# Block sums of a weight moved to the first wave, a seven-product step in one more wave, loads in one row and gated casts

## The chip, the cores and the metric

One core of one Trainium2 chip. The kernel is one launch; its time is device microseconds (us), from the runs of that one core. Three runs of the kernel before gave 197.93, 197.23 and 197.22 us, median 197.23. All other times come from one profiled execution. Its span, from the first instruction to the last, is 196.2 us, and that execution took 197.88 us as a whole.

Engines: PE (TensorE, matrix products), DVE (VectorE), ACT (ScalarE), POOL (GpSimd), SP (SyncE, which here only issues transfers). "SPq" in a row is SP's queue of transfer issues.

## The reference, cut to what matters

A decayed linear attention over 4 batches of 8 heads, 768 positions, head size 64, feeds a two-layer network of 3072 tokens, 512 to 2048 to 512:

```
for b in range(nb):                       # 64 positions at a time
    intra = (einsum(qb, kb) * Dmask) @ vb
    inter = (qb * lam_pow) @ kv_state
    out[:, :, sl] = intra + inter
    kv_state = lam_block * kv_state + einsum(kb * rev_pow, vb)
...
x = out.transpose(0, 2, 1, 3).reshape(B * S, H * D)
h = x @ w_in
g = h * sigmoid(1.702 * h)
return g @ w_out
```

## The kernel before

The work runs in six waves of 512 tokens, w = 0 to 5. Waves 0 and 1 hold two batches with 256 positions each; waves 2 to 5 hold all four batches with 128 positions each. Wave w does the network for its own tokens, and in between the attention of wave w+1, so that its input xT is there when the next wave begins.

**The first product** (x @ w_in, 16 blocks of 128 columns). A plain block, `mlp1`, is four matmuls of 512 columns. The other form works on a group of four blocks and half blocks of x (256 tokens): seven products (`in_product`, n = 1 to 7, two columns of blocks, two steps each, so four matmuls of 256 columns a product) in place of eight, in the manner of Strassen and Winograd. It needs two sorts of sums made by DVE: four sums of blocks of w_in for each group (`in_sums(g)`, lines 510 to 519, kept in the tiles `w_in_t`), and four sums of half blocks of x for each wave (`x_sums`, line 528, tiles `x_s`). After the products DVE or ACT copy three of the seven banks to `part`, DVE adds the others up (line 551, `h_sb`), and ACT takes the activation (line 562). `GR[w]` names the groups that wave w does in this form; before, wave 2 does groups 2 and 3 so and the other eight blocks plain, waves 3 to 5 do all four groups so. Which group holds which blocks is in `GROUPS`; w_in is loaded in five chunks (`IN_CH`), groups 1, 2 and 3 lie in chunks 0 to 3, group 0 in chunks 1 and 4.

**The second product** (g @ w_out) takes the seven-product form from wave 1 on (`product`, line 460; sums of g by DVE in `g_sums`, line 439; results added by DVE at line 484 or copied by ACT at 482, then stored by SP, lines 490 and 492). Wave 0's second product is plain (`mlp2`), its stores are issued late, in wave 1 (line 580).

**Attention of waves 2 to 5**: k and q are loaded (`load`, line 88), multiplied by powers (`do_cast`, line 209; on DVE for wave 2, on POOL for waves 3 to 5: the steps K0, K1, Q0, Q1), turned by a transposing DMA that SP issues (`turn_dma`, line 245: tk0, tk1, tq0, tq1), then come the scores (S0 to S3, line 335), masks (M or m), states and outputs (R), and the copy to xT. v is cast by ACT (v0, v1).

**What sets the order.** In waves 0 and 1 a list of main items (products) runs with a list of side items, each with the number of the main item ahead of which it is placed: `IN_SUMS_AT`, `X_AT`, `L_AT` are such places in wave 1. Main item 12 of wave 1 is a plain block, item 26 and 27 are the two halves of product 4, 28 and 29 of product 3. In waves 2 to 5 the order is written out by hand in `STEPS`: lower-case a to d with a number is a product of group 1 to 4 of that wave, capital A to D an activation, f a plain block, i the sums of w_in of one group, P a product of the second layer, g its sums, o the output of product 2, X the sums of x for the next wave, L the loads for the wave after the next (Lk: k and q, Lv: v). Each engine runs its instructions in this order and each waits only for what it needs; SP's loads, turns and stores share one queue in this order too.

Buffers that matter: k and q are loaded into one buffer each, v into two. `h_sb`, `o_sb` share a tag of six buffers; a buffer is free again when its add, activation or store has been done.

Of the kernel before, what the change touches and what calls it, by code (L numbers as in the profile page):

```python
# [25 lines left out]
def kernel(  # L26
# [21 lines left out]
    G = W // P  # L48
# [194 lines left out]
    def turn_dma(w, c, nm):  # L243
        y = work.tile([P, 2 * NP, P], bf16, tag=f"{nm}T{c}", bufs={"k": 1, "q": 2}[nm], name=f"{nm}T")
        nc.sync.dma_start_transpose(out=y, in_=cast[w, c, nm].rearrange("p b c -> p (b c)"))
        trans[w, c, nm] = y
# [149 lines left out]
    def mlp1(w, fc):  # L396
        if w not in g_of:
            g_of[w] = gp.tile([P, FFC, W], bf16, tag="g", name="g_sb")
        j, i = w_in_of[fc]
        h = acc("ps_h", shape=[P, W], tag="mm")  # L400
        for kc in range(KC):
            nc.tensor.matmul(h, w_in_sb[j][:, kc, i * P : (i + 1) * P], xT[w][:, kc, :],  # L402
                             start=(kc == 0), stop=(kc == KC - 1))
        nc.scalar.activation(g_of[w][:, fc, :], h, GELU)  # L404
# [88 lines left out]
                out=out.rearrange("(b s) d -> s b d", s=S)[w * P : (w + 1) * P, 2 * i + t.start : 2 * i + t.stop, cols],  # L493
                in_=o[:, t])

    GR = {w: (2, 3) if w == 2 else (1, 2, 0, 3) for w in range(2, 6)}
    TAGS = {w: ("aQXV", "aXVQ") if w == 2 else ("aQXV", "mXVQ", "aQXV", "aXVQ") for w in range(2, 6)}
    IN_SUMS_AT, X_AT, L_AT = ((13.5, 2), (26.5, 3)), 28.5, ((12, "v"), (24, "kq"))
    GROUPS = (((4, 13), (14, 15)), ((0, 2), (1, 3)), ((6, 5), (8, 7)), ((10, 9), (12, 11)))
    USED = sorted({g for w in range(NW) for g in GR.get(w, ())})  # L500
    TI = {g: [const.tile([P, KC // 2, 2, P], bf16, name=f"w_in_t{g}{n}") for n in range(1, 5)] for g in USED}
    x_sum, h_part, h_bank, h_out = {}, {}, {}, {}

    def in_half(g, kh, j, u):
        ch, i = w_in_of[GROUPS[g][u][j]]
        return w_in_sb[ch][:, 2 * kh : 2 * kh + 2, i * P : (i + 1) * P]

    def in_pair(g, kh, j):
        (ch, a), (_, b) = (w_in_of[GROUPS[g][u][j]] for u in range(2))
        return w_in_sb[ch].rearrange("p kc (i f) -> p kc i f", f=P)[:, 2 * kh : 2 * kh + 2, a : b + 1 : b - a]  # L510

    def in_sums(g):
        whole_pair = all(w_in_of[GROUPS[g][0][j]][0] == w_in_of[GROUPS[g][1][j]][0] for j in range(2))
        for u in (None,) if whole_pair else (0, 1):
            t1, t2, t3, t4 = (t if u is None else t[:, :, u] for t in TI[g])
            b11, b12, b21, b22 = (in_pair(g, kh, j) if u is None else in_half(g, kh, j, u)
                                  for kh in range(2) for j in range(2))
            for o, x, y in ((t1, b12, b11), (t2, b22, t1), (t3, b22, b12), (t4, b21, t2)):
                nc.vector.tensor_tensor(o, x, y, op=SUB)  # L519
# [38 lines left out]
    def in_gelu(w, g, n, bank=None):  # L558
        bank = bank or h_out.pop((w, g, n))
        i, j = {2: (0, 0), 3: (0, 1), 4: (1, 0), 5: (1, 1)}[n]  # L560
        a, b = (GROUPS[g][u][j] for u in range(2))
        nc.scalar.activation(g_of[w][:, a : b + 1 : b - a, 256 * i : 256 * i + 256], bank, GELU)  # L562
# [30 lines left out]
    def one_step(w, s):  # L593
        if s[0] == "+":
            w, s = w + 1, s[1:]
        x, a = w + 1, s[1:]
        if s[0] == "f":
            mlp1(w, int(a))
        elif s[0] in "abcd":
            k = "abcd".index(s[0])  # L600
            in_product(w, GR[w][k], int(s[1]), TAGS[w][k], dve_copy if s[2:] == "v" else act_copy)
        elif s[0] in "ABCD":
            in_gelu(w, GR[w]["ABCD".index(s[0])], int(a))
        elif s[0] == "P":
            product(w, int(s[1]), (int(s[2]),))
        elif s[0] in "kq":
            do_cast(x, int(a), s[0], nc.vector)
        elif s[0] in "KQ":
            do_cast(x, int(a), s[0].lower(), nc.gpsimd)
        elif s[0] == "t":  # L610
            turn_dma(x, int(s[2]), s[1])
        elif s[0] == "v":
            cast_v(x, int(s[1]), ((act_copy, dve_copy)[s[2:] == "v"],))
        elif s[0] == "S":
            n_scores(x, int(a))
        elif s[0] == "M":
            n_masks(x, int(a))
        elif s[0] == "m":
            n_masks(x, int(a), True)
        elif s[0] == "R":  # L620
            n_rest(x)
        elif s[0] == "o":
            c11.pop(w)()
        elif s[0] == "X":
            x_sums(x)
        elif s[0] == "i":
            in_sums(int(a))
        elif s[0] == "g":
            m0, m1 = {"l": (0, 4), "h": (4, 8)}[s[1]]
            g_sums(w, m0, m1, tuple(int(c) - 1 for c in s[2:]))  # L630
        elif s[0] == "L":
            load(w + 2, {"v": "v", "k": "kq"}[a])
        else:
            raise ValueError(s)

    STEPS = {
        2: ("f0 f1 a1 f2 a7 a2 i1 f3 K0 tk0 b1 a6 b7 i0 f4 A2 a5 b2 b6 K1 tk1 a4 A5 f13 a3 A4 B2 b5 gl12 Q0 "
            "tq0 b4 f14 B5 b3 B4 Q1 tq1 Lv f15 gl3 P10 P11 gh31 S0 S1 M0 P20 M1 gh2 P21 v0 P70 P71 S2 S3 M2 "
            "M3 v1 o P60 gl4 gh4 P61 Lk R P50 P51 P40 X P41 P30 P31 "),
        3: ("a1 a7v a2 a6 K0 tk0 b1 b7v A2 a5 b2 b6 a4 A5 a3 c1 A4 K1 tk1 B2 b5 c7v c2 c6 B5 b3 b4 d1v Q0 "  # L640
            "tq0 c5 B4 C2 d7v d2 d6 D2 c3 c4 Q1 tq1 Lv d5 d4 P10 C4 d3 C5 D4 P11 gl3 D5 gh3 S0 S1 M0 P20 m1 "
            "gl1 P70 P71 gl2 P21 v0 gh12 S2 S3 M2 m3 v1 o P40 P60 gl4 gh4 P61 Lk R P50 P51 X P41 P30 P31 "),
        4: ("a1 a7v a2 a6 K0 tk0 b1 b7v A2 a5 b2 b6 a4 A5 a3 c1 A4 K1 tk1 B2 b5 c7v c2 c6 B5 b3 b4 d1v Q0 "
            "tq0 c5 B4 C2 d7v d2 d6 D2 c3 c4 Q1 tq1 d5 d4 P10 C4 d3 C5 D4 P11 gl3 D5 gh3 S0 S1 M0 P20 m1 gl1 "
            "P70 P71 gl2 P21 v0 gh12 S2 S3 M2 m3 v1 o P40 P60 gl4 gh4 P61 R P50 P51 X P41 P30 P31 "),
        5: ("a1 a7v a2 a6 b1 b7v A2 a5 b2 b6 a4 A5 a3 c1 A4 B2 b5 c7v c2 c6 B5 b3 b4 d1v c5 B4 C2 d7v d2 d6 "
# [4 lines left out]
    def gate_pool(x):  # L651
        nc.gpsimd.tensor_copy(behind_q, x)
# [4 lines left out]
    with tc.manual_schedule():  # L657
# [87 lines left out]
        side, main = [(0, (end, 0, 1))], []  # L745
        for w in range(ND):
            n = len(main)
            main += mlp_items(w)
            e = len(main)
            x = w + 1  # L750
            if x < ND:
                for c, (k_at, q_at, v_at, k_turn, q_turn, s_at, e_at) in enumerate(
                        ((19, 20, 19, 24, 25.5, 27, 30), (26.5, 28, 28, 29, 30, 32, 34))):
                    side += [(n + k_at, (do_cast, x, c, "k", (nc.vector, nc.gpsimd)[c])),
                             (n + q_at, (do_cast, x, c, "q", nc.vector)),
                             (n + v_at, (cast_v, x, c, ((pool_copy, pool_copy), (act_copy, act_copy))[c])),
                             (n + k_turn, (turn_pe, x, c, "k", act_copy)),
                             (n + q_turn, (turn_pe, x, c, "q", act_copy)),
                             (n + s_at, (start, x, c)), (n + e_at, (end, x, c))]
            elif x == ND:  # L760
                for c in range(HF):
                    tk, tq = n + 2.1 + 2 * c, n + 4 + c
                    side += [(tk, (do_cast, x, c, "k", nc.vector)), (tk, (turn_dma, x, c, "k")),
                             (tq, (do_cast, x, c, "q", nc.vector)), (tq, (turn_dma, x, c, "q")),
                             (n + 17 + 2 * c, (cast_v, x, c, (act_copy,)))]
                side += [(n + 7, (stores,))]
                side += [(n + 16, (n_two, x, 0)), (n + 20, (n_two, x, 1)), (n + 24, (n_rest, x))]
                side += [(n + t, (in_sums, g)) for t, g in IN_SUMS_AT] + [(n + X_AT, (x_sums, x))]
            if w == 0:
                side += [(n + 14, (weight_sums, j)) for j in range(NCH - 1)]  # L770
            else:
                side += [(n + 7.5, (weight_sums, NCH - 1))]
                side += [(n + 8.9, (g_sums, w, 0, 4)), (n + 12.9, (g_sums, w, 4, 6)), (n + 15.9, (g_sums, w, 6, 8))]
            side += [(n + 12, (load, w + 2))] if w == 0 else [(n + t, (load, w + 2, nms)) for t, nms in L_AT]
# [8 lines left out]
        for w in range(ND, NW):  # L783
            for s in STEPS[w].split():
                one_step(w, s)
# [30 lines left out]
```

## Time and profile before

| what | value |
|---|---|
| median of three runs | 197.23 us |
| the profiled execution: whole, span | 197.88 us, 196.2 us |
| PE busy | 188.5 us (96%) |
| DVE busy | 147.3 us (75%) |
| ACT busy | 120.4 us (61%) |
| POOL busy | 42.7 us (22%) |
| granted TensorE clock | 1.00 throughout |
| a plain block of four 512-column matmuls, start to start | 0.86 us |
| a product of four 256-column matmuls, start to start | 0.44 us |
| starts of the first product of waves 2, 3, 4, 5 on PE | 80.97, 111.51, 139.93, 168.38 us |

A matmul is pipelined: its row shows a duration longer than the distance to the next one, so distances between starts are what counts on PE. Times in views are us from the span's start. In a row of the timeline of an engine, the first number is the start, the second the length of the row, "xN" the instructions merged in it, and the bracket the idle time before it with what ended it.

### The profile page before, as it was taken

What the parts mean: (1) busy time and instruction counts of PE and PEld (TensorE: products, weight loads), DVE (VectorE), ACT (ScalarE), POOL (GpSimd) and SP (SyncE); (2) the same over time, 40 slices, a digit from 0 to 9 for tenths busy, and PEclk for the clock granted to TensorE, in tenths of its full rate; (3) what the DMA queues carried; (4) which work ended last, traced back from release to release, by engine and by line L of the source; (5) the groups of instructions that cost most, each with busy time, mean ns of one, the idle gap of its engine ahead of it and who ended that gap; (6) DMA issues with size and microseconds to landing.
All of it is one profiled execution on the core that took longest, in us unless ns stands there. A gap on an engine that the chain in (4) does not pass through costs nothing.

```text
span 196.2 us, 5312 instructions
## 1 busy us (share of the span) xinstructions
PE 188.5 (96%) x2201; PEld 142.7 (73%) x2201; DVE 147.3 (75%) x277; ACT 120.4 (61%) x225; POOL 42.7 (22%) x62
## 2 busy tenths in 40 slices
PE   7999999999999999997999999999999899999993
PEld 2567544456784789764788888878888788888882
DVE  1795036288799894999899679799879796789850
ACT  4958663056676725374946278895288975487711
POOL 4579000051000000891000294000392000000000
PEclk9999999999999999999999999999999999999999
DMA  5999999999998699998902999953999101400113
GB/s 145 335 248 188 202 205 223 271 295 269 244 235 199 144 226 241 211 234 194 212 5 68 214 288 176 223 113 87 231 307 212 27 0 57 160 5 0 34 62 122
DMA packets 89086, 33.90 MB, mean 173 GB/s; under 512 B 67430, under 2 KB 88422, under 8 KB 89062
## 3 DMA queue, kind: packets, MB, share of 16 engines
q1 hardware_dynamic: 84164, 28.84, 62.5%
q0 software_dynamic: 4896, 4.72, 14.4%
q8 instruction: 17, 0.28, 0.6%
q14 instruction: 7, 0.06, 0.1%
q10 hardware_dynamic: 2, 0.00, 0.0%
HBM read 27.26 MB, written 6.29 MB: 171 GB/s over the span
## 4 chain that ended last, share of the span: by engine, by line
PE 67%; DMA 18%; DVE 7%; SPq 2%; POOL 2%; ACT 1%; issue 1%; DVEq 0%; ACTq 0%
PE ps_X L460 17%; PE ps_hX L543 10%; PE ps_V L460 8%; DMA w_out<-in_moe_w_out_dram 7%; PE ps_h L402 6%; PE ps_hV L543 5%; PE ps_Q L460 4%; PE ps_h L414 4%; DMA kf<-in_k_dram 4%; PE ps_out L571 3%; DMA vf<-in_v_dram 3%; PE ps_hQ L543 3%; DVE w_in_t L519 3%; DMA qT<-qs 3%; DMA qf<-in_q_dram 2%; PE ps_o L390 2%
## 5 line engine op out<-in xcount | busy, mean ns | idle before, releaser
L460 PEld LDWEIGHTS <-g_s 128*128 128x128 bf16 x320 | 30.6, 98 | 4.6 <-DVE g_s L439 0.4
L209 POOL TENSOR_TENSOR ks<-kf,k_pow 128x512 bf16<-128x512 f32 x12 | 12.8, 1094 | 77.7 <-DMA kf<-in_k_dram 43.1
L562 ACT ACTIVATE g_sb<-h_sb 128x512 bf16<-128x512 f32 x42 | 25.5, 634 | 1.3 <-DVE h_sb L551 1.2
L402 PE MATMUL ps_h<-xT,w_in 128*128 128x512 bf16 x112 | 25.6, 379 | 0.0
L460 PEld LDWEIGHTS <-g_sb 128*128 128x128 bf16 x240 | 22.9, 98 | 3.5
L543 PEld LDWEIGHTS <-w_in_t 128*128 128x128 bf16 x224 | 21.9, 98 | 3.3 <-issue 0.3
L404 ACT ACTIVATE g_sb<-ps_h 128x512 bf16<-128x512 f32 x28 | 16.7, 597 | 6.9 <-PE ps_h L402 6.8
L543 PEld LDWEIGHTS <-w_in 128*128 128x128 bf16 x168 | 16.4, 98 | 4.4 <-issue 1.7
L460 PE MATMUL ps_X<-w_out_t,g_s 128*128 128x256 bf16 x160 | 19.3, 273 | 0.1
L402 PEld LDWEIGHTS <-w_in 128*128 128x128 bf16 x112 | 11.0, 98 | 11.3
L221 ACT COPY part<-ps_hX 128x512 f32<-128x512 f32 x25 | 14.3, 589 | 7.7 <-PE ps_hX L543 4.8
L439 DVE TENSOR_TENSOR g_s<-g_sb 128x1024 bf16<-128x1024 bf16 (+1 forms) x22 | 13.9, 638 | 4.8 <-ACT g_sb L562 4.1
L543 PE MATMUL ps_hX<-x_s,w_in_t 128*128 128x256 bf16 x112 | 16.8, 272 | 0.1
L348 DVE SCALAR_TENSOR_TENSOR sm<-ps_s,inv_pow,mask 128x512 bf16<-128x512 f32 x24 | 16.5, 742 | 0.2 <-PE ps_s L335 0.2
L482 ACT COPY o_sb<-ps_X 128x512 f32<-128x512 f32 (+1 forms) x6 | 3.1, 515 | 19.5 <-PE ps_X L460 19.5
L571 PE MATMUL ps_out<-w_out,g_sb 128*128 128x512 bf16 x64 | 14.8, 379 | 0.0
L209 POOL TENSOR_TENSOR qs<-qf,q_pow 128x512 bf16<-128x512 f32 x12 | 12.9, 1094 | 0.4 <-DVE w_in_t L519 0.3
L221 ACT CAST v_sb<-vf 128x1024 bf16<-128x1024 f32 (+1 forms) x13 | 11.3, 884 | 1.3 <-DMA vf<-in_v_dram 1.3
L426 DVE TENSOR_TENSOR w_out_t<-w_out 128x512 bf16<-128x512 bf16 x8 | 3.4, 420 | 10.8 <-DMA w_out<-in_moe_w_out_dram 10.8
L218 DVE COPY part<-ps_hV 128x512 f32<-128x512 f32 x12 | 8.2, 687 | 4.2 <-PE ps_hV L543 4.2
L414 PE MATMUL ps_h<-xT,w_in 128*128 128x256 bf16 x96 | 11.4, 273 | 0.0
L551 DVE TENSOR_TENSOR h_sb<-part,ps_hX 128x512 f32<-128x512 f32 x14 | 9.5, 680 | 2.1 <-PE ps_hX L543 1.2
(114 smaller groups left out, 355.4 us busy)
## 6 DMA issues: line engine op xcount, KB each, us to landing
kf<-in_k_dram SPq DMA_DIRECT2D x10, 512.0 KB, 6.5
qf<-in_q_dram SPq DMA_DIRECT2D x10, 512.0 KB, 6.2
vf<-in_v_dram SPq DMA_DIRECT2D x10, 512.0 KB, 6.1
out_dram<-o_sb SPq DMA_DIRECT2D x24, 128.0 KB, 2.6
out_dram<-o_sb SPq DMA_DIRECT2D x12, 256.0 KB, 3.2
w_out<-in_moe_w_out_dram POOLq DMA_DIRECT2D x4, 512.0 KB, 13.9
kf<-in_k_dram SPq DMA_DIRECT2D x4, 256.0 KB, 3.0
qf<-in_q_dram SPq DMA_DIRECT2D x4, 256.0 KB, 4.5
```

Of the source, the lines that this page charges most:

```text
L209: eng.tensor_tensor(x.rearrange("p b (r i j d) -> p j (b r) i d", i=2, j=2, d=D)[:, j], f.rearrange("p h (a d) -> p (h a) d", a=2).rearran ...
L221: nc.scalar.copy(out, in_)
L348: nc.vector.scalar_tensor_tensor(sm, s, inv_pow[:, n : n + 1], mask.to_broadcast([P, B, P]), op0=MUL, op1=MUL)
L402: nc.tensor.matmul(h, w_in_sb[j][:, kc, i * P : (i + 1) * P], xT[w][:, kc, :], start=(kc == 0), stop=(kc == KC - 1))
L404: nc.scalar.activation(g_of[w][:, fc, :], h, GELU)
L414: nc.tensor.matmul(h[:, u, :], w_in_sb[j][:, kc, i * P : (i + 1) * P], xT[w][:, kc, cols], start=(kc == 0), stop=(kc == KC - 1))
L439: nc.vector.tensor_tensor(o, x, y, op=f)
L460: nc.tensor.matmul(bank[:, t], x[:, m, t * P : (t + 1) * P], y, start=(n in (1, 2, 7) and t == ts[0] * last and m == 0), stop=(m == FFC // ...
L543: nc.tensor.matmul(bank[:, u], z[:, kc], y[:, kc], start=(n in (1, 2, 7) and u + kc == 0), stop=(kc == 1), skip_group_check=True)
L551: nc.vector.tensor_tensor(h, h_part[w, g, {2: 1, 5: 7, 4: 6}[n]], bank, op=ADD)
L562: nc.scalar.activation(g_of[w][:, a : b + 1 : b - a, 256 * i : 256 * i + 256], bank, GELU)
L571: nc.tensor.matmul(ps_out, g_of[w][:, fc, g * P : (g + 1) * P], w_out_sb[j][:, fc % CW, :], start=(fc == 0), stop=(fc == FFC - 1))
```

## The change

- `GR`, `TAGS`: wave 2 does all four groups in the seven-product form, in the order of wave 3; its plain blocks (f steps) go.
- `IN_SUMS_AT`: `in_sums` for groups 1, 2, 3, 0 stands in wave 0, ahead of main items 5, 6, 7 and 10. Before, groups 2 and 3 stood in wave 1 (13.5 and 26.5), groups 1 and 0 in wave 2 (steps i1, i0, which go).
- `X_AT`: the sums of x for wave 2 stand at 26.5 of wave 1 in place of 28.5.
- `L_AT`: in wave 1, k and q of wave 3 are loaded at 12 and v at 12.5; before, v at 12, k and q at 24.
- In the steps of waves 2 and 3, Lk and Lv stand together behind tq1, the last turn. Before, Lv stood there, and Lk late in the wave, behind P61.
- A new step G ahead of K0 in waves 2, 3 and 4: POOL copies one element of the last sum of x of this wave, so that its casts start behind these sums.

```diff
-    GR = {w: (2, 3) if w == 2 else (1, 2, 0, 3) for w in range(2, 6)}
-    TAGS = {w: ("aQXV", "aXVQ") if w == 2 else ("aQXV", "mXVQ", "aQXV", "aXVQ") for w in range(2, 6)}
-    IN_SUMS_AT, X_AT, L_AT = ((13.5, 2), (26.5, 3)), 28.5, ((12, "v"), (24, "kq"))
+    GR = {w: (1, 2, 0, 3) for w in range(2, 6)}
+    TAGS = {w: ("aQXV", "mXVQ", "aQXV", "aXVQ") for w in range(2, 6)}
+    IN_SUMS_AT, X_AT, L_AT = ((5, 1), (6, 2), (7, 3), (10, 0)), 26.5, ((12, "kq"), (12.5, "v"))
...
-        elif s[0] == "i":
-            in_sums(int(a))
+        elif s[0] == "G":
+            gate_pool(x_sum[w][3][0:1, 0, 0:1])
...
-        2: ("f0 f1 a1 f2 a7 a2 i1 f3 K0 tk0 b1 a6 b7 i0 f4 A2 a5 b2 b6 K1 tk1 a4 A5 f13 a3 A4 B2 b5 gl12 Q0 "
-            "tq0 b4 f14 B5 b3 B4 Q1 tq1 Lv f15 gl3 P10 P11 gh31 S0 S1 M0 P20 M1 gh2 P21 v0 P70 P71 S2 S3 M2 "
-            "M3 v1 o P60 gl4 gh4 P61 Lk R P50 P51 P40 X P41 P30 P31 "),
-        3: ("a1 a7v a2 a6 K0 tk0 b1 b7v A2 a5 b2 b6 a4 A5 a3 c1 A4 K1 tk1 B2 b5 c7v c2 c6 B5 b3 b4 d1v Q0 "
-            "tq0 c5 B4 C2 d7v d2 d6 D2 c3 c4 Q1 tq1 Lv d5 d4 P10 C4 d3 C5 D4 P11 gl3 D5 gh3 S0 S1 M0 P20 m1 "
-            "gl1 P70 P71 gl2 P21 v0 gh12 S2 S3 M2 m3 v1 o P40 P60 gl4 gh4 P61 Lk R P50 P51 X P41 P30 P31 "),
...
+        2: ("a1 a7v a2 a6 G K0 tk0 b1 b7v A2 a5 b2 b6 a4 A5 a3 c1 A4 K1 tk1 B2 b5 c7v c2 c6 B5 b3 b4 d1v Q0 "
+            "tq0 c5 B4 C2 d7v d2 d6 D2 c3 c4 Q1 tq1 Lk Lv d5 d4 P10 C4 d3 C5 D4 P11 gl3 D5 gh3 S0 S1 M0 P20 "
+            "m1 gl1 P70 P71 gl2 P21 v0 gh12 S2 S3 M2 m3 v1 o P40 P60 gl4 gh4 P61 R P50 P51 X P41 P30 P31 "),
+        3: ...
...
-                side += [(n + t, (in_sums, g)) for t, g in IN_SUMS_AT] + [(n + X_AT, (x_sums, x))]
+                side += [(n + X_AT, (x_sums, x))]
             if w == 0:
+                side += [(n + t, (in_sums, g)) for t, g in IN_SUMS_AT]
```

Wave 4's steps gain only the G. The copy that G calls:

```
def gate_pool(x):
    nc.gpsimd.tensor_copy(behind_q, x)
```

## The prediction, made before the change was run

> **What bounds the kernel now.** I read the page's shares first, then the busy time by stretches, one per wave, then PE's timeline and the chain of waits at PE's longest pause, and last the timelines of DVE and SP there.
>
> ```profile
> PE 188.5 (96%) x2201; PEld 142.7 (73%) x2201; DVE 147.3 (75%) x277; ACT 120.4 (61%) x225; POOL 42.7 (22%) x62
> ```
>
> PE is busy 96% at a granted clock of 1.00, so time goes only if PE has fewer matmuls or a pause closes. The next view has stretch, length, then busy us of PE, PEld, DVE, ACT, POOL:
>
> ```profile
> 80.97:95.77 14.80, 13.35 (x91) 8.60 (x89) 13.74 (x24) 10.19 (x20) 7.68 (x7) 1.00 0.91 217
> 95.77:111.51 15.74, 15.74 (x242) 13.56 (x241) 15.01 (x27) 7.66 (x13) 0.00 (x0) 1.00 0.44 102
> 111.51:139.93 28.42, 28.32 (x355) 24.41 (x352) 24.28 (x44) 20.74 (x37) 8.14 (x8) 1.00 0.90 185
> 139.93:168.38 28.45, 27.89 (x322) 24.01 (x320) 23.02 (x41) 20.74 (x37) 8.17 (x8) 1.00 0.63 132
> ```
>
> The first two are wave 2 (first product, then the rest), then waves 3 and 4. Wave 2 takes 14.80 + 15.74 = 30.54 us, wave 3 takes 28.42. PE's pause in wave 2, from PE's timeline, and its cause in the chain of waits (start, us, what) and in DVE's timeline:
>
> ```profile
> 92.06 0.60 PE L543 MATMUL ps_hX<-x_s,w_in 128*128 128x256 bf16 x4 [1.38 <-DVE h_sb L551]
> ```
>
> ```profile
> 85.43 0.68 DVE h_sb L551
> 86.11 0.60 DVE w_in_t L519
> ...
> 86.73 3.03 DVE w_in_t L519 x4
> ...
> 89.78 0.91 DVE w_in_t L519 x4
> ```
>
> ```profile
> 81.28 1.86 DVE L528 TENSOR_TENSOR x_s<-xT 128x512 bf16<-128x512 bf16 x2
> 83.17 1.15 DVE L528 TENSOR_TENSOR x_s<-x_s,xT 128x512 bf16<-128x512 bf16 x1
> 84.36 1.15 DVE L528 TENSOR_TENSOR x_s<-xT,x_s 128x512 bf16<-128x512 bf16 x1
> ...
> 86.73 1.29 DVE L519 TENSOR_TENSOR w_in_t<-w_in,w_in_t 128x512 bf16<-128x512 bf16 x1
> 87.95 1.26 DVE L519 TENSOR_TENSOR w_in_t<-w_in 128x512 bf16<-128x512 bf16 x1
> ```
>
> DVE is busy 13.74 of 14.80 us there, with the sums of x and of w_in. These run while POOL casts (from 79.42): sums of x take 81.28 to 85.51 there, 4.2 us, but 108.89 to 110.56, 1.7 us, ahead of wave 3, where POOL is idle. The second pause is in wave 4: a score waits 0.54 us for q's last turn, issued at 149.95 and landing 4.97 later.
>
> ```profile
> 154.96 0.51 PE L335 MATMUL ps_s<-qT,kT 64*128 64x128 bf16 x12 [0.54 <-DMA qT<-qs]
> ```
>
> **The change, part by part.**
>
> *Wave 2, first product.* Eight plain blocks (the chain has eight in wave 1 from 58.49, 6.91 in all, 0.864 each) become two groups of seven products. Wave 3 has 27 products from 111.51 to 123.34, 0.438 each; 14 are 6.13. PE saves 6.91 − 6.13 = 0.78. All 28 then take 12.27 against 14.80 now: 2.53 saved, of which 0.78 is work, 1.38 the pause, and 0.37 is smaller gaps around it.
>
> *Wave 2, rest.* It takes wave 3's order. Wave 3 from 123.34, less its one remaining product (0.44), is 16.59 − 0.44 = 16.15 against 15.74: 0.41 lost, because wave 3's PE waits a little for DVE's sums of g (its product row at 131.21 lasts 2.18 where others last 1.91) and for the bank of its last product. Bounds: 0 to 0.41; I take 0.41, since the instructions will be the same as wave 3's. So wave 2 gains 30.54 − 28.42 = 2.12.
>
> *Sums of w_in in wave 0.* DVE is idle there between two rows, 18.62 and 27.45, waiting for w_out:
>
> ```profile
> 17.93 0.69 DVE L218 CAST xT<-ps_o 128x512 bf16<-128x512 f32 x1 [1.37 <-PE ps_o L298]
> 27.45 0.42 DVE L426 TENSOR_TENSOR w_out_t<-w_out 128x512 bf16<-128x512 bf16 x1 [8.83 <-DMA w_out<-in_moe_w_out_dram]
> ```
>
> Groups 1, 2, 3 are four instructions each (64.08 to 65.63 for one group: 1.55), group 0 is eight of half size (89.47 to 91.41: 1.94): 3 × 1.55 + 1.94 = 6.6 us into 8.83. They wait for chunks of w_in; the last chunk's issue ends its row at 16.23, so starts near 15.5, and the longest landing in that line's view is 9.2: 24.7. Group 0 then ends at 26.6, before 27.45. Cost 0. If chunks came 3 us later, the sums of w_out would slip from 34.05 to some 37, still before DVE's casts at 37.84, which wait for a load. POOL is idle from 19.51 to 40.92, so nothing slows these. In wave 1 the removed sums free DVE, but PE pauses nowhere in that wave: 0.
>
> *Sums of x at 26.5.* They need xT (ACT's copies end at 76.71) and then follow DVE's add that ends at 78.44: 1.65 us, to 80.1, before PE's start of wave 2 at 80.97. Behind them on DVE waits only product 4's add, 80.68 now, 80.1 then. Gain counted above.
>
> *G.* POOL's copy took 0.33 (row at 6.91). Behind it on POOL stand the four casts, 8.25 us (111.59 to 119.80), then the turns and scores. Wave 2: K0 at 80.4 instead of 79.42, last cast done at 88.7. Waves 3 and 4: the sums of x of wave 4 end 0.2 us ahead of its start, so K0 starts 0.2 us after it, about as now (0.08 and 0.34): 0. Without the gate, POOL would meet these sums: 4.2 − 1.7 = 2.5 us longer on DVE. The page "SBUF — State Buffer" of the Trainium skill, section "Who interferes with whom", says that a DVE instruction with two inputs in SBUF and a reading GpSimd instruction shut each other out for a whole instruction. By it, four sums against four casts of 1.05 us would cost up to 4.2 us more on DVE without the gate, by the row 2.5; neither enters the sum, as the gate is there.
>
> *Loads in one row.* In waves 2 and 3 the loads leave the stretch ahead of the next wave's turns. In wave 4 SP now issues loads till 142.14 and stores till 145.50 ahead of the first turn (145.61), though K0 was done at 142.3. Then the last turn can go out when its cast is done, 148.4, and not at 149.95; 4.97 later is 153.4, before the score needs it (154.14 + 0.29). The 0.54 goes. Bounds: 0 (another late landing) to 0.64 (28.45 − wave 3's 28.42 without its 0.61 of state products); I take 0.50.
>
> *The row in wave 1* is the dear part. SP's queue now:
>
> ```profile
> 68.09 2.14 SPq L88 DMA_DIRECT2D vf<-in_v_dram  x2
> 70.87 2.24 SPq L490 DMA_DIRECT2D out_dram<-o_sb  x2
> 73.16 2.70 SPq L88 DMA_DIRECT2D kf<-in_k_dram  x2
> 75.91 5.05 SPq L88 DMA_DIRECT2D qf<-in_q_dram  x2
> 81.05 5.46 SPq L490 DMA_DIRECT2D out_dram<-o_sb  x6
> 86.62 2.69 SPq L245 DMA_TRANSPOSE kT<-ks  x2
> 89.43 2.58 SPq L245 DMA_TRANSPOSE qT<-qs  x2
> ```
>
> Six loads go out from 68.09. At best 2.14 + 2.70 + 5.05 = 9.9, to 78.0; at worst as the six from 40.89 to 54.00, 13.1, to 81.2. I take 79, as a pair after stores costs 2.14. Eight stores follow, at 5.46/6 each: 7.3, to 86.3; four turns, the last issued 4.1 later at 90.4 (its cast done 88.7), landing 2.7 to 5.0 later: 93.1 to 95.4. Scores are due at 80.97 + 14.11 (125.62 − 111.51) = 95.08. Also, of six `h_sb`/`o_sb` buffers, the third add of wave 2 (b2, due at 80.97 + 4.03 = 85.0) gets that of product 2's output, whose store now waits behind the row: 79 + 5.8 (that line's longest landing) = 84.8. So 0 at best. At worst (row to 81.2) the turn lands at 92.6 + 5.0 = 97.6, a wait of 2.5. Nearest to the rows: 0.1.
>
> The page "DMA: Bandwidth & Descriptors", in its opening table, says that transfers under 512 B fall below line rate because each is a read-modify-write. It speaks against a longer row of these loads, but gives no price; here six of 512 KB took 13.1 us, which is the upper bound already used.
>
> *Sum* on the profiled execution: −2.53 + 0.41 − 0.50 + 0.10 = −2.52, span 196.2 to 193.7. That execution took 197.88, the median is 197.23; the wait in wave 4 (0.54) may be just what sets them apart. With that term the median would go to 194.7, without it to 195.2. I take 195.0.
>
> **The rivals.**
> - *The row costs part of it.* Stores behind six loads land late, DVE waits at b2's add, and PE loses 0.7 to 1.5 us. For it: 84.8 against 85.0 is no margin. Against: DVE has 0.61 idle soon after in wave 3, and the buffer is P2's alone. 195.7 to 196.2.
> - *The row takes all of it.* At the upper bound, 2.5 us at the scores, −2.02 + 2.5: some 197.7 at most; no change.
> - *Slower: SP's queue becomes the bound of wave 2.* The row ends at 81.2 and each store costs what the longest in its line did, 1.71: 8 × 1.71 = 13.7, to 94.9; last turn issued at 99, landing at 101.7, and scores wait 6.6: 197.23 − 2.02 + 6.6 = 201.8. It decides once q's last turn lands after 95.08 + 2.02 + 0.99 = 98.1. Against: only the first store behind loads costs 1.71, others 0.62.
> - *The change doesn't do what it says:* DVE, not the sums, holds wave 2, now with 12 adds in place of 6. Then wave 2 stays near 30 us: 196.7. Against: wave 3 does the same at 24.28 busy of 28.42 without a pause.
>
> **How the numbers follow.** Forecast 0.72, own range 194.1 (2.53 + 0.64 gained) to 195.7. Part of it lost 0.12. Gain gone, by the row or by DVE, 0.07. Slower 0.09. A change under 0.5%, 0.99 us, can't be told from none, so the bounds are 196.24 and 198.22. Faster 0.72 + 0.12 = 0.84, same 0.07, slower 0.09. The range 194.1 to 196.3 leaves out the last two cases.
>
> **What would show it.** PE starts wave 2 near 81, its 28 products follow without a pause, wave 3 starts near 109.4. DVE makes all w_in sums between 18.6 and 27.4; the sums of x take 1.7 us and end before 80.97. POOL's first cast of wave 2 starts near 80.4. The scores of wave 4 don't wait. Wrong, if scores of wave 2 wait for a turn, if an add waits for a store, or if DVE is still at w_in sums when w_out has landed.

## The result, and the profile after

The changed kernel's median is 195.25 us (194.37 to 197.03, 17 runs), that of the kernel before on the same occasions 197.65 us (196.82 to 199.5, 17 runs). The ratio is 0.9885, 95% interval 0.9853 to 0.9917, so it is faster by 1.15% (0.83 to 1.47%), some 2.3 us. The forecast was 195.0, range 194.1 to 196.3. Medians are of all runs; ratios, here and below, are of the runs in the chip's faster and usual state alone.

The profiled execution of the changed kernel took 197.03 us, the longest of its 17 runs, with a span of 195.3, only 0.9 us under the profiled execution before. Read whole, the two profiles would show less than half of the gain. Read by waves they don't. Busy time by stretches, changed kernel, one stretch for each of waves 2 to 5 (from PE's first matmul of a wave to that of the next). The columns are stretch, length, busy us of PE, PEld (PE's weight loads), DVE, ACT and POOL, then the granted clock of PE, the busy share of the transfer engines and GB/s:

```profile
82.40:111.22 28.82, 28.55 (x355) 24.42 (x353) 24.10 (x44) 20.78 (x37) 7.49 (x9) 1.00 0.93 220
111.22:139.62 28.40, 28.30 (x354) 24.42 (x352) 24.62 (x45) 20.71 (x37) 8.21 (x10) 1.00 0.80 187
139.62:167.53 27.91, 27.81 (x323) 23.87 (x321) 23.06 (x41) 20.71 (x37) 8.15 (x9) 1.00 0.31 77
167.53:195.30 27.77, 24.64 (x226) 21.68 (x223) 18.30 (x32) 15.57 (x32) 0.00 (x0) 1.00 0.17 58
```

Wave 2 went from 30.54 to 28.82, wave 3 stayed at 28.4, wave 4 went from 28.45 to 27.91: 2.28 us less together. But wave 2 begins at 82.40 and not at 80.97. That 1.4 us lies in wave 0 (36.1 us from PE's first block of the first product to wave 1, against 34.6 before), and the runs below show that it belongs to the execution and not to the change.

The sums of w_in on DVE's timeline, changed kernel:

```profile
19.41 0.41 DVE L519 TENSOR_TENSOR w_in_t<-w_in,w_in 128x512 bf16<-128x512 bf16 x1
...
24.45 0.42 DVE L519 TENSOR_TENSOR w_in_t<-w_in 128x512 bf16<-128x512 bf16 x1 [1.80 <-DMA w_in<-in_moe_w_in_dram]
...
26.45 0.29 DVE L519 TENSOR_TENSOR w_in_t<-w_in,w_in 128x256 bf16<-128x256 bf16 x1 [0.45 <-DMA w_in<-in_moe_w_in_dram]
...
28.12 0.28 DVE L519 TENSOR_TENSOR w_in_t<-w_in,w_in_t 128x256 bf16<-128x256 bf16 x1
28.97 0.42 DVE L426 TENSOR_TENSOR w_out_t<-w_out 128x512 bf16<-128x512 bf16 x1 [0.57 <-DMA w_out<-in_moe_w_out_dram]
```

They wait for chunks of w_in twice, end at 28.40, and DVE still waits 0.57 us for w_out: they are hidden. Sums of x ahead of wave 2, and the opening of the gate on POOL's timeline:

```profile
79.78 0.75 DVE L528 TENSOR_TENSOR x_s<-xT 128x512 bf16<-128x512 bf16 x2
80.57 0.43 DVE L528 TENSOR_TENSOR x_s<-x_s,xT 128x512 bf16<-128x512 bf16 x1
81.03 0.43 DVE L528 TENSOR_TENSOR x_s<-xT,x_s 128x512 bf16<-128x512 bf16 x1
```

```profile
81.59 0.18 POOL L652 CAST behind_q<-x_s 1x1 f32<-1x1 bf16 x1 [35.31 <-DVE x_s L528]
81.73 4.06 POOL L209 TENSOR_TENSOR ks<-kf,k_pow 128x512 bf16<-128x512 f32 x4
```

The sums take 1.7 us where they took 4.2, end 0.9 us ahead of the wave, and the casts begin behind them. In wave 4 the scores no longer wait: sixteen matmuls in one row, with no idle time ahead of them. SP's last turn of this wave is issued 8.18 us into it (147.80); before, it was 10.02 us into it (149.95).

```profile
153.72 0.62 PE L335 MATMUL ps_s<-qT,kT 64*128 64x128 bf16 x16
```

```profile
141.76 3.24 SPq L245 DMA_TRANSPOSE kT<-ks  x2
147.80 1.77 SPq L245 DMA_TRANSPOSE qT<-qs  x1
```

One pause is new. From PE's timeline, the chain of waits ahead of it, and the add in that chain on DVE's timeline:

```profile
89.30 0.60 PE L543 MATMUL ps_hX<-x_s,w_in_t 128*128 128x256 bf16 x4 [0.16 <-ACT part L221]
```

```profile
87.89 0.70 DVE h_sb L551
...
88.66 0.59 ACT part L221
...
89.30 1.12 PE ps_hX L543 x8
```

```profile
87.89 0.69 DVE L551 TENSOR_TENSOR h_sb<-part,ps_hQ 128x512 f32<-128x512 f32 x1 [1.37 <-PE ps_hX L543]
```

DVE's add for b2 starts at 87.89, 5.49 us after the wave's start; in wave 3 the same add came 4.03 after it. ACT's copy and PE's product wait behind. This is the 0.42 by which wave 2 is longer than wave 3. The row names a product on PE as what ended the wait. It is the one that starts 4.83 us into the wave, and the add does not need it: in the second profile of this kernel (e1 below) the add started at 4.03, ahead of that product. What the add needs is a buffer, that of product 2's output. SP's queue shows how late product 2's store (the first two of eight at line 490) went out:

```profile
69.45 2.22 SPq L88 DMA_DIRECT2D kf<-in_k_dram  x2
71.71 4.83 SPq L88 DMA_DIRECT2D qf<-in_q_dram  x2
76.58 4.55 SPq L88 DMA_DIRECT2D vf<-in_v_dram  x2
81.24 7.39 SPq L490 DMA_DIRECT2D out_dram<-o_sb  x8
88.74 2.67 SPq L245 DMA_TRANSPOSE kT<-ks  x2
91.54 2.58 SPq L245 DMA_TRANSPOSE qT<-qs  x2
```

The longest landing of this line, 6.2 us, is that of its first store: from 81.24 to 87.4, 0.5 us ahead of the add.

### The profile page after: what moved, and what is told of

The parts are those of the page before. It is cut to its first block, busy times and chain, and to the rows that moved or that the text cites. A ratio compares the mean times of both kernels' runs of the same rounds, so it can differ in the third digit from the quotient of the medians.

```text
span 195.3 us, 5379 instructions
## 1 busy us (share of the span) xinstructions
PE 187.3 (96%) x2218; PEld 144.4 (74%) x2225; DVE 148.3 (76%) x288; ACT 123.5 (63%) x230; POOL 42.0 (21%) x65
## 3 DMA queue, kind: packets, MB, share of 16 engines
q1 hardware_dynamic: 84164, 28.84, 59.7%
## 4 chain that ended last, share of the span: by engine, by line
PE 66%; DMA 16%; DVE 10%; ACT 3%; POOL 2%; issue 1%; SPq 1%; ACTq 0%; DVEq 0%
PE ps_X L460 17%; PE ps_hX L543 14%; PE ps_hV L543 7%; DMA w_out<-in_moe_w_out_dram 7%; DVE g_s L439 5%; PE ps_V L460 5%; PE ps_h L414 4%; DMA vf<-in_v_dram 4%; PE ps_h L402 4%; PE ps_hQ L543 3%; DMA kf<-in_k_dram 3%; PE ps_out L571 3%; DMA qf<-in_q_dram 3%; ACT g_sb L562 2%; PE ps_o L390 2%; DVE sm L348 2%
## 5 line engine op out<-in xcount | busy, mean ns | idle before, releaser
L562 ACT ACTIVATE g_sb<-h_sb 128x512 bf16<-128x512 f32 x48 | 29.1, 632 | 1.4 <-DVE h_sb L551 1.4
L543 PEld LDWEIGHTS <-w_in_t 128*128 128x128 bf16 x256 | 25.0, 98 | 3.4 <-issue 0.3
L221 ACT COPY part<-ps_hX 128x512 f32<-128x512 f32 x28 | 16.0, 588 | 6.9 <-PE ps_hX L543 6.5
L543 PE MATMUL ps_hX<-x_s,w_in_t 128*128 128x256 bf16 x128 | 19.2, 272 | 0.2 <-ACT part L221 0.2
L402 PE MATMUL ps_h<-xT,w_in 128*128 128x512 bf16 x78 | 17.5, 379 | 0.1
L404 ACT ACTIVATE g_sb<-ps_h 128x512 bf16<-128x512 f32 x20 | 11.9, 597 | 5.3 <-PE ps_h L402 5.3
L218 DVE COPY part<-ps_hV 128x512 f32<-128x512 f32 x16 | 11.0, 688 | 5.2 <-PE ps_hV L543 5.2
L348 DVE SCALAR_TENSOR_TENSOR sm<-ps_s,inv_pow,mask 128x512 bf16<-128x512 f32 x20 | 13.9, 743 | 0.0
L551 DVE TENSOR_TENSOR h_sb<-part,ps_hX 128x512 f32<-128x512 f32 x16 | 10.9, 680 | 1.9 <-ACT g_sb L562 1.9
L551 DVE TENSOR_TENSOR h_sb<-part,ps_hQ 128x512 f32<-128x512 f32 x16 | 10.9, 679 | 1.4 <-PE ps_hX L543 1.4
```

The lines of the kernel that those rows point to most:

```text
L218: nc.vector.tensor_copy(out, in_)
L221: nc.scalar.copy(out, in_)
L348: nc.vector.scalar_tensor_tensor(sm, s, inv_pow[:, n : n + 1], mask.to_broadcast([P, B, P]), op0=MUL, op1=MUL)
L543: nc.tensor.matmul(bank[:, u], z[:, kc], y[:, kc], start=(n in (1, 2, 7) and u + kc == 0), stop=(kc == 1), skip_group_check=True)
L551: nc.vector.tensor_tensor(h, h_part[w, g, {2: 1, 5: 7, 4: 6}[n]], bank, op=ADD)
```

## The experiments

Lengths of waves by PE's starts, in us, one profiled execution each. "Wave 0" runs from PE's first block of the first product to that of wave 1. Where the record of a wave's first matmul is missing (e2 and f2, the two kernels with plain blocks in wave 2 and sums in wave 0), the start is taken 1.74 after that of product 3, as in the others.

| kernel | wave 0 | wave 1 | wave 2 | wave 3 | wave 4 |
|---|---|---|---|---|---|
| before | 34.64 | 31.59 | 30.54 | 28.42 | 28.45 |
| changed | 36.09 | 31.59 | 28.82 | 28.40 | 27.91 |
| e1 changed again | 36.76 | 31.59 | 28.40 | 28.41 | 27.90 |
| e2 sums only | 34.13 | 31.58 | 28.77 | 28.67 | 28.47 |
| e4 no gate | 34.38 | 31.59 | 32.72 | 33.86 | 27.90 |
| f1 base, turns as copies | 34.09 | 31.59 | 28.40 | 28.41 | 27.90 |
| f2 plain blocks in wave 2 | 34.24 | 31.59 | 28.77 | 28.40 | 27.90 |
| f3 old loads in wave 1 | 34.10 | 31.59 | 28.40 | 28.40 | 27.90 |
| f4 m1 late | 34.63 | 31.59 | 29.35 | 29.35 | 28.84 |

### e1: the changed kernel once more

> The changed kernel once more. My theory: the change acts between PE's start of wave 2 and its start of wave 5 only, and the 1.4 us by which its profiled execution was late at wave 2 (82.40 against 80.97) belong to that execution's loads at the start, not to the change. Then waves 2, 3, 4 again take 28.8, 28.4, 27.9 us, and the start of wave 2 may lie anywhere from 80.5 to 82.5. Rival: the sums in wave 0 delay wave 0 or 1; then wave 2 starts at 82 or later again.

Measured: ratio to before 0.9871 (0.9832 to 0.9910). The profiled execution was again the longest, 197.46 us; the six others took 194.32 to 195.04. Waves 3 and 4 are the same to 0.01; wave 2 took 28.40 this time, without the new pause: its store left at 81.34, 1.89 us ahead of PE's start of wave 2 (83.23), where in the first profile it left 1.16 ahead. Wave 2 began late again, at 83.23 and so past the 82.5 that the theory allowed, and by the expectation's own words that speaks for the rival; e2 and e4 decide against it, since both make the same sums in wave 0 and their wave 0 took 34.13 and 34.38, less than before's 34.64, as did those of f1 to f4 (34.09 to 34.63).

### e2: the sums of w_in alone

```diff
-    IN_SUMS_AT, X_AT, L_AT = ((13.5, 2), (26.5, 3)), 28.5, ...
+    IN_SUMS_AT, X_AT, L_AT = ((5, 1), (6, 2), (7, 3), (10, 0)), 28.5, ...
-        2: ("f0 f1 a1 f2 a7 a2 i1 f3 ... b7 i0 f4 ...
+        2: ("f0 f1 a1 f2 a7 a2 f3 ... b7 f4 ...
+                side += [(n + t, (in_sums, g)) for t, g in IN_SUMS_AT]
```

> The kernel before, with the sums of w_in for its two groups (2 and 3) and for groups 1 and 0 made in wave 0 and nothing else changed; wave 2 keeps eight plain blocks. My theory: the pause of 1.38 and the gaps around it go with the sums of w_in, so wave 2 takes 30.54 less 1.4 to 1.8, some 28.9 us, and wave 4 keeps its wait of 0.5 for a turn: 1.5 us faster than before. Rival: the pause comes from POOL's casts slowing DVE (sums of x at 1.0 us apiece); then the sums of x still end past wave 2's start and wave 2 takes over 29.6.

Measured: ratio 0.9947 (0.9914 to 0.9979), about 1 us (0.4 to 1.7) where 1.5 was expected; the profiles by waves give 1.50. Stretches of waves 2, 3 and 4, and the two pauses of PE:

```profile
80.63:109.40 28.77, 28.66 (x328) 22.18 (x328) 22.95 (x37) 18.07 (x32) 6.61 (x6) 1.00 0.68 158
109.40:138.07 28.67, 28.33 (x355) 24.54 (x353) 24.29 (x44) 20.74 (x37) 8.18 (x8) 1.00 0.92 191
138.07:166.54 28.47, 27.86 (x322) 24.02 (x320) 23.04 (x41) 20.73 (x37) 8.10 (x8) 1.00 0.59 128
```

```profile
124.14 0.51 PE L335 MATMUL ps_s<-qT,kT 64*128 64x128 bf16 x12 [0.34 <-DMA qT<-qs]
153.12 0.51 PE L335 MATMUL ps_s<-qT,kT 64*128 64x128 bf16 x12 [0.61 <-DMA qT<-qs]
```

Moving the sums takes 1.77 us off wave 2, of the 2.14 by which e1's is shorter than before's. The sums of x were still slowed here, with the loads and the place of before and without the gate (4.6 us from 79.70), and PE did not pause: the pause was DVE's sums of w_in, not the sums of x. So the rival falls. Waves 3 and 4 wait for turns, 0.34 and 0.61, with the loads in their old places: in wave 4 the last turn is issued 10.38 us into the wave, behind loads and stores, against 8.18 in the changed kernel. The three profiles with turns and the loads in one row (the changed kernel, e1, e4) show no such wait. As e4 has no gate, it is not the gate that removed it; the loads of waves 2 and 3 alone were not moved in any run.

### e4: without the gate

```diff
-        2: ("a1 a7v a2 a6 G K0 ...
+        2: ("a1 a7v a2 a6 K0 ...
```

The `G` of waves 3 and 4 goes too.

> The changed kernel without the step G. My theory: POOL casts as soon as k has landed, some 5 us or more ahead of each wave, and meets DVE's sums of x and g: the four sums of x take 3.5 to 5 us instead of 1.7, and waves lose 0.5 to 2 us together. Rival: early casts cost PE nothing, since the sums of x have slack; then waves 2 to 4 take the same within 0.2 us each.

Measured: median 206.27 us, ratio 1.0423 (1.0366 to 1.0480): 4% slower than before, and by ratios 5.4% slower than the changed kernel. Waves 2 and 3 took 32.72 and 33.86, 9.8 us more than e1's, where the theory had put 0.5 to 2. Busy time in these two stretches:

```profile
80.30:113.02 32.72, 29.80 (x355) 24.95 (x353) 30.31 (x46) 20.62 (x37) 10.62 (x9) 0.95 0.80 191
113.02:146.88 33.86, 30.03 (x355) 25.19 (x352) 29.29 (x45) 20.72 (x37) 10.25 (x8) 0.95 0.72 157
```

DVE, 24.10 busy in the changed kernel's wave 2, is now 30.31 with the like number of instructions, and PE stands still for 2.9 us of its 32.72. DVE's sums of g in wave 2 and PE's waits for them:

```profile
98.58 0.68 DVE L439 TENSOR_TENSOR g_s<-g_sb 128x1024 bf16<-128x1024 bf16 x1
99.30 1.42 DVE L439 TENSOR_TENSOR g_s<-g_s,g_sb 128x1024 bf16<-128x1024 bf16 x1
100.64 1.53 DVE L439 TENSOR_TENSOR g_s<-g_sb 128x1024 bf16<-128x1024 bf16 x1
102.21 1.42 DVE L439 TENSOR_TENSOR g_s<-g_s,g_sb 128x1024 bf16<-128x1024 bf16 x1
```

```profile
100.78 0.61 PE L460 MATMUL ps_X<-w_out_t,g_s 128*128 128x256 bf16 x4 [0.63 <-DVE g_s L439]
103.68 2.74 PE L460 MATMUL ps_X<-w_out_t,g_s 128*128 128x256 bf16 x12 [2.30 <-DVE g_s L439]
```

```profile
98.99 2.63 POOL L209 TENSOR_TENSOR ks<-kf,k_pow 128x512 bf16<-128x512 f32 x2 [0.95 <-PE ps_s L335]
101.59 5.14 POOL L209 TENSOR_TENSOR qs<-qf,q_pow 128x512 bf16<-128x512 f32 x4
```

The sums of x ahead of wave 2 do meet casts, as the theory has it, and take 3.7 us (77.69 to 81.41), but PE doesn't pause for them. The loss comes later. With k and q landed early, POOL casts in the second half of the wave, and meets the sums of g, which PE needs at once: 0.68 us for the one that starts ahead of the casts, 1.42 to 1.53 beside them. The listed waits are 2.9 of the 4.3 us that wave 2 loses against e1's. The rest lies right behind them, where the granted clock is 0.50, in wave 2 as in wave 3:

```profile
103.68:106.35 2.67, 2.67 (x12) 1.64 (x12) 2.67 (x4) 0.00 (x0) 2.67 (x3) 0.50 0.97 220
137.30:139.97 2.67, 2.67 (x12) 1.64 (x12) 2.67 (x6) 0.00 (x0) 0.00 (x0) 0.50 0.00 0
```

Twelve such matmuls take 1.31 us at the usual 0.44 for four, so each wave loses 1.36 there: 2.93 + 1.36 = 4.29. In wave 3 the waits are 2.26 and 1.57. A pause alone does not tell whether the clock falls: behind the 1.38 us in wave 2 of the kernel before it stayed at 1.00. The page "SBUF — State Buffer" of the Trainium skill, section "Who interferes with whom", has a DVE instruction with two SBUF inputs and a reading GpSimd instruction shut each other out. The doubled rows of DVE agree in kind; the loss is not shared evenly, as the casts went only from 1.03 us each (2.06 for two at 72.00) to 1.29 (5.14 for four).

This run also bears on the new pause of the changed kernel. The add for b2 on DVE's timelines, first in e4, then in e1:

```profile
85.01 0.69 DVE L551 TENSOR_TENSOR h_sb<-part,ps_hQ 128x512 f32<-128x512 f32 x1 [0.41 <-DMA out_dram<-o_sb]
```

```profile
87.26 0.68 DVE L551 TENSOR_TENSOR h_sb<-part,ps_hQ 128x512 f32<-128x512 f32 x1
```

In e4 the add waits for a transfer out of `o_sb`, 4.71 us after the wave's start (80.30). Store issued ahead of the wave's start, and add after it: 1.16 and 5.49 (changed), 1.58 and 4.71 (e4), 1.89 and 4.03 (e1), 4.27 and 4.04 (f1). The earlier the store, the sooner the add, down to some 4.03, which is also what wave 3 has. The landings agree: with the longest of its line, the store is done at 84.6 in e4 (5.9 us), 0.4 ahead of the add, and at 86.4 in e1 (5.1 us), before the add is due. More buffers would have tested this directly, but eight in place of six do not fit (24 KB per partition, 20.7 are left).

### f1: the base for three more

The turns are plain copies here and in f2 to f4; those kernels leave out the turning of k and q. The same edits to the kernel with its turns were not measured.

```diff
-        nc.sync.dma_start_transpose(out=y, in_=cast[w, c, nm].rearrange("p b c -> p (b c)"))
+        nc.sync.dma_start(out=y, in_=cast[w, c, nm].rearrange("p b (r s) -> p (b r) s", s=P))
```

> The changed kernel with one substitution, the base for the next three: the transposing DMAs of k and q in waves 2 to 5 are plain copies of the same bytes, so the turning is left out and the scores are of unturned tiles. Nothing on PE, DVE, ACT or POOL changes. Theory: waves 2, 3, 4 take 28.4 to 28.8, 28.4, 27.9 as in the changed kernel, since none of them waits for a turn. Rival: if the turns held up PE in a way that the profile doesn't name, the waves get shorter by more than 0.2.

Measured: ratio to before 0.9888 (0.9863 to 0.9913). Waves 2, 3 and 4 took 28.40, 28.41 and 27.90: what e1 took with its turns. In f1 PE shows no idle row from wave 0 on, and no score of the changed kernel has one for a turn; a wait that turns and copies share would not show in this comparison.

### f2: plain blocks kept in wave 2

```diff
-    GR = {w: (1, 2, 0, 3) for w in range(2, 6)}
+    GR = {w: (2, 3) if w == 2 else (1, 2, 0, 3) for w in range(2, 6)}
...
+        2: ("f0 f1 a1 f2 a7 a2 f3 G K0 tk0 b1 a6 b7 f4 A2 ... Q1 tq1 Lk Lv f15 gl3 P10 P11 gh31 S0 S1 M0 ...
```

> As f1, but wave 2 keeps its eight plain blocks and its old order (sums in wave 0, loads in one row, gates and the sums of x at 26.5 as changed). It parts the worth of the seven-product form from the rest. Theory by the prediction: plain blocks cost 0.78 us more of PE, the old order of the rest saves 0.41, so wave 2 takes some 28.8, 0.4 over 28.4. Rival: the form is worth its full 0.78 and wave 2 takes 29.2; or nothing, and wave 2 takes 28.4 or less, as DVE's adds cost what PE saves.

Measured: ratio 0.9880 (0.9850 to 0.9910), no different from f1's; whole times, with intervals of 0.5% and 0.6%, can't tell 0.4 us. Its wave 2 in two stretches, first product and rest:

```profile
80.40:93.43 13.03, 12.93 (x89) 8.61 (x89) 4.93 (x8) 10.84 (x21) 7.42 (x8) 1.00 0.78 214
93.43:109.17 15.74, 15.74 (x242) 13.56 (x240) 14.40 (x26) 7.22 (x13) 0.81 (x2) 1.00 0.76 184
```

13.03 + 15.74 = 28.77, against 12.26 + 16.14 = 28.40 in f1 (27 products from 80.60 to 92.42, and one of 0.44): by stages the form is worth 0.37 in wave 2, 0.77 in the first product less 0.40 that wave 3's order of the rest costs. DVE is busy 4.93 of 13.03 us in the first product here, so it has room there. Most of the 0.40 is a wait for DVE's sums of g: in the changed kernel's wave 2 product 6's weights wait 0.4 for them, and its row lasts 2.19 where others last 1.91. The rest was not parted.

### f3: wave 1's loads where they were

```diff
-    ... 26.5, ((12, "kq"), (12.5, "v"))
+    ... 26.5, ((12, "v"), (24, "kq"))
```

> As f1, with wave 1's loads where they were before (v at 12, k and q at 24), so that product 2's store goes out ahead of k and q. Theory: the add for b2 in wave 2 waits for no store and comes 4.0 us after the wave's start; wave 2 takes 28.4. Rival: k lands after the gate has opened, casts and turns of wave 2 end late, and its scores wait 0.5 us or more; or b2 waits still, so it wasn't the store.

Measured: ratio 0.9877 (0.9851 to 0.9903), waves as f1's to 0.01. Product 2's store left at 70.29 and b2's add came at 4.03, but f1 had no wait either: with copies in place of turns, its loads left at 64.67 and not at 69.45. The run says that with copies the row in wave 1 brings nothing over the old places, and does not tell whether the old places would have spared the changed kernel its pause.

### f4: an attempt at the rest's 0.41

```diff
-   ... P20 m1 gl1 P70 P71 gl2 P21 v0 gh12 S2 S3 ...
+   ... P20 gl1 P70 P71 gl2 P21 v0 gh12 m1 S2 S3 ...
```

> As f1, with the step m1 behind gh12 in waves 2, 3 and 4, so that DVE makes the sums of g that product 6 needs 0.67 us earlier. Theory: product 6's pause of 0.27 us a wave (a row of 2.19 where others last 1.91) goes, since it waits for these sums: waves 2, 3 and 4 each take 0.2 to 0.3 less than f1's. Rival: the pause moves to the outputs (step R), whose masks now come last on DVE; then the waves take the same.

Measured: ratio 1.0032 (1.0000 to 1.0064), 2.8 us over f1 by waves. Product 6's row is 1.91 again, as the theory has it, though PE also comes to it a microsecond later, as the scores now wait:

```profile
100.15 0.38 PE L335 MATMUL ps_s<-qT,kT 64*128 64x128 bf16 x7 [1.01 <-ACT sm L344]
100.46 1.05 PE L460 MATMUL ps_V<-w_out_t,g_sb 128*128 128x256 bf16 x8
101.35 1.91 PE L460 MATMUL ps_X<-w_out_t,g_s 128*128 128x256 bf16 x16
```

m1 has two halves, ACT's scaling, which empties the banks (of PE's output memory) that hold the scores, and DVE's mask. Moving the step moved both, and the next scores waited for ACT's half, 1.01 us. Both theory and rival fall; the attempt would have to move DVE's half alone, which was not tried. None of these runs beats the changed kernel.

## Why the prediction was right

- *First product and rest of wave 2*: 12.27 and 16.15 were put; f1 has 12.26 and 16.14. f1 and f2 show the two terms of the form apart, 0.77 and 0.40, where 0.78 and 0.41 were worked out. e2 shows that the moved sums carry 1.77 of the 2.14.
- *Sums of w_in hidden in wave 0*: as put, with 0.57 us to spare in the profile where 0.85 was worked out.
- *Sums of x, gate's copy, casts*: 1.65 put, 1.68 measured; the gate's copy cost 0.18, not 0.33.
- *Loads out of the way of wave 4's turns*: −0.50 put, −0.54 measured, and a wait of 0.61 with old loads in e2. The last turn was to go out at 148.4, 8.5 us into the wave; it went out 8.2 into it. The wait stood in e2 too, so it is hardly what set the profiled execution of before apart from the median, as the forecast half supposed.
- *The row in wave 1*: six loads took 11.7 us of SP's queue (put: 10.9, bounds 9.9 and 13.1), eight stores 7.4 (put: 7.3). The scores of wave 2 did not wait. b2's add did, in one profile of two, and PE lost 0.42 and 0 where 0.10 was put. An add that waits for a store was named as a sign of being wrong, and the first rival's way of losing 0.7 to 1.5; it came, at a smaller price.
- *The sum*: −2.52 put. By waves the profiles give −2.28 (the first) and −2.70 (e1), the medians −2.40, the ratio −2.3. The forecast of 195.0 stood for −2.2 on a base of 197.23. It was picked between 194.7 and 195.2, and the base was 0.42 higher on these occasions, so that it missed by only 0.25 us is in part luck. The differences by waves are not. The rivals' −2.02 still holds the 0.10 of the row and leaves out the 0.50 of wave 4, which moves their times by half a microsecond and decides nothing.
- *Mis-sized*: what the gate is worth. It was put at 2.5 us of DVE at the sums of x; taking it away cost 9.8 us over two waves, as the casts then meet the sums of g: 6.8 us of PE's waits, and most of the rest at a granted clock of 0.50 behind them. That was the step with the wrong size. The step looked only at the place of before's collision, and not at where early loads would let the casts go. It was no term of the sum.
- *What would show it*: wave 2 was to start near 81 and wave 3 near 109.4. They started at 82.40 and 111.22, and with them the first cast (81.73 for 80.4) and the last of the sums of w_in (28.40 for 27.4) came late, for want of the remark that wave 0 differs by over a microsecond from one execution to the next. The 28 products of wave 2 were to follow without a pause, and had one.

## What to carry to other kernels

Work that needs only weights belongs in the stretch where its engine waits for data anyway: here that took 1.77 us off one wave, while a cheaper algorithm for the same product gave half of its 0.77 us back in the work behind it. Loads that come earlier set free the work behind them, so ask what that work will run beside; here they would have cost 9.8 us without a one-element copy as a gate. The gate is no gain over the kernel before; it is what makes the early loads harmless. When two profiles differ less than their medians, compare them by stages before looking for a lost gain.

## What the runs showed that was not expected

Wave 0 took 34.09 to 36.76 us in nine profiles, and the two longest are the changed kernel's. In its first profile PE waited for late loads: 0.78 us for the cast of the first v, which began on POOL at 15.90 and in seven of the others at 14.01 to 14.65, and 0.48 and 0.28 us for DVE's casts of k, which had waited for their load. In e1's profile PE waited 0.98 for w_in, and then the granted clock was low:

```profile
18.95:23.24 4.29, 4.29 (x24) 3.15 (x25) 3.13 (x8) 1.20 (x2) 1.41 (x3) 0.60 1.24 198
```

The same 24 matmuls took 2.68 us in f1. So with a wait of one microsecond for a load PE lost 2.6 in all. Why the loads at the start differ from one execution to the next is not shown. The median of before moved by 0.7 us between occasions (196.97 to 197.65), nearly a third of what was measured here.
